# Retention attention and a gated linear unit on one core: stores on ScalarE's queue, a second batch of queries by chunk, output weights in one load, zero products in the waits

## The chip, the core and the metric

The kernel runs on one core of a Trainium2 chip. A core has a matrix engine (TensorE, in the profile PE, with its weight loads as PEld), VectorE (DVE), ScalarE (ACT), GpSimd (POOL) and SyncE (SP), which here only issues transfers. Each engine takes its instructions in the order of the program. Engines wait for each other through semaphores. Sixteen DMA engines move data between HBM and the on-chip memory SBUF. Products of the matrix engine land in PSUM, from where VectorE or ScalarE take them. The metric is the time of one execution in device microseconds; less is better. The time before is 179.71 us, the median of three runs (178.24 to 180.51).

## The reference

Inputs are `q`, `k`, `v` of 8 batches, 8 heads, 576 tokens and 64 values a head, in float32, two 512 x 512 matrices `w_val` and `w_out` and five convolution taps for each of 512 channels.

```python
scores = scale * np.matmul(q, k.transpose(0, 1, 3, 2))
gamma = 1.0 - 2.0 ** (-5.0 - np.arange(H))
Dmat = np.where(rel >= 0, gamma[:, None, None] ** rel[None], 0.0)   # rel = i - j
x = np.matmul(scores * Dmat, v)            # heads side by side: (B, S, 512)
gate_pre = sum(conv_w[k] * xp[:, k:k + S, :] for k in range(5))  # causal, zeros ahead
out = (1 / (1 + np.exp(-gate_pre)) * (x @ w_val)) @ w_out
```

So a linear attention with a decay per head is followed by a gated unit: the gate is a causal convolution over tokens within each channel, the value a full product, and the output again a full product.

## The kernel before, in words

**Chunks.** The tokens of a batch are cut into four chunks of 128 and a tail of 64. Tails of two batches make one chunk. With eight batches there are 36 chunks, in the list `chunks`: batches 0 to 3 by chunk (0 to 15), two tail chunks (16, 17), and the same for batches 4 to 7 (18 to 35).

**Attention of a chunk `t`.** The key tile is cast to bfloat16 (`cast_k`, on GpSimd from chunk 3 on) and turned on the matrix engine with a copy back out of PSUM on VectorE (`turn_k`). Values are cast and weighted with the decay (`cast_v`). Queries are cast (`cast_q`) and turned (`turn_q`, copy on ScalarE unless told otherwise). All turned tiles go through the one PSUM buffer `tps`. `scores` makes the products of keys and queries, `masks` multiplies them with the causal mask on VectorE, `values` adds the products with the values to what `carried` has put there: the products of the queries with the state of the chunks before. `update` adds keys times values to the state in PSUM; `take_state` casts it into SBUF on ScalarE. `take_x` brings the result, with the outgoing decay `gout`, into the tile `xg`.

**Unit `n`.** Two chunks, 2n and 2n + 1, make a unit of the gated part: `conv` (40 small products with diagonal matrices, L379), `gate` (two sigmoids on ScalarE, L387), `value` (two groups of eight products, L394, and the multiplication with the gate on VectorE) and `project` (two groups of four products with `wob`, L405, a copy to SBUF on ScalarE, L408, and a store, L411, or L414 for tails). All these share three PSUM buffers named `g`.

**Loads.** Keys and values come by chunk (`load`, L78 and L81), 256 KB each in pieces of 256 bytes. The queries of batch 0 and of the tails come by chunk as well. The queries of the other batches come as one load of 1 MB (`load_queries`, L94) with pieces of 1 KB: partition p then holds tokens 4p to 4p + 3, so the turned queries have another token order, which `mask_q`, `queries` and `take_x` account for. There are nine buffers for keys and for values (`LA` + 1), two for batch queries.

**Order.** The order is written out by hand (`manual_schedule`): each engine's queue follows the order of the calls. Chunks 0 to 3 with units 0 and 1 stand line by line ahead of a loop (L442 to L531). The loop from L533 runs over `t`: it issues the load of chunk t + 6, casts for later chunks, then `scores` and `masks` of t + 1, `values` of t, in even steps `conv` and `gate` of unit n = t/2 - 1, then `turn_k` of t + 2, half a `value` or `project`, the turned query tiles that `qjobs` lists for this step, the other half, and `carried` and `update` of t + 1. All loads and nearly all stores are issued by SP, so a store that waits for its tile holds up the loads behind it, as does a long issue.

**Zero products.** `keep_warm(n)` issues n products of zeros (L437), 512 columns wide. Before the change they stand only at the very start.

**Output weights.** The convolution leaves half of the channel blocks with their 64-row halves exchanged. `wob` therefore has the rows of `w_out` exchanged in the same way; three loads (L109 to L111) bring the rows to their places, and `prep_wo` (L198) only casts.

Of the kernel before, what the change touches and what calls it, by code (L numbers as in the profile page):

```python
# [21 lines left out]
def kernel(  # L22
# [20 lines left out]
    LA = 8  # L43
    RQ = NCH
    assert D == 64 and DM == H * D and TAIL == 64 and B % GB == 0 and NP == 4
# [24 lines left out]

    with tc.manual_schedule():
# [34 lines left out]

        wof = consts.tile([P, 2, 2, DM], F32, name="wof")
        wo_src = moe_w_out.rearrange("(pr ab hl p) n -> ab hl p pr n", pr=2, ab=2, hl=2)
# [89 lines left out]
        def prep_wo(copy, i):  # L198
            rows, blk, ab = ((slice(0, 64), 0, 0), (slice(64, 128), 0, 1), (slice(0, 64), 2, 1), (slice(64, 128), 2, 0))[i]
            copy(wob[rows, blk:blk + 2], wof[rows, ab])  # L200
# [75 lines left out]
        def masks(t, i):  # L276
            kind, b, c = chunks[t]
            m = mask_t if kind == "tail" else mask if b == 0 else mask_q
# [36 lines left out]
        def take_x(t):  # L315
# [3 lines left out]
            if kind == "full":  # L319
                i0 = c * P  # L320
                if b == 0:
                    nc.vector.tensor_tensor(x[:, bl, :, PAD + i0:PAD + i0 + P], ops[t], gout[:, :, i0:i0 + P], op=ALU.mult)  # L322
                    return
# [76 lines left out]
        def project(n, i):  # L400
            kind, b, c = chunks[2 * n]
            last = n == NT // 2 - 1
            o = ps_g.tile([P, DM], F32, name="g")
            for j in range(NP):
                nc.tensor.matmul(o, lhsT=zsb[n, j // 2][:, j % 2, i * P:(i + 1) * P], rhs=wob[:, j, :],  # L405
                                 start=(j == 0), stop=(j == NP - 1))
            ob = op_sb.tile([P, DM], F32, name="ob")
            nc.scalar.copy(ob, o)  # L408
            if kind == "full":
                c0 = (c + i) * P  # L410
                nc.sync.dma_start(out=out[b, c0:c0 + P, :], in_=ob)  # L411
            else:
                for j in range(2):
                    (nc.scalar if last and j else nc.sync).dma_start(out=out[b + 2 * i + j, NCH * P:S, :], in_=ob[j * TAIL:(j + 1) * TAIL])  # L414
# [8 lines left out]
        for b in range(B - 1, 1, -1):  # L423
            fit = [s for s in range(3, start_of[b] - 1) if s not in qjobs][-RQ:]
            for r, s in enumerate(fit):
                qjobs[s] = [("batch", b, r)]
        qload = {}
# [4 lines left out]
        v_copy, g_copy, s_copy = nc.vector.tensor_copy, nc.gpsimd.tensor_copy, nc.scalar.copy  # L432
        idle = ps_g.tile([P, DM], F32, name="g")

        def keep_warm(n):
            for _ in range(n):
# [87 lines left out]
        cast_k(4)  # L524
        turn_q(("batch", 1, 1), v_copy)
        cast_v(4)
        turn_k(4)
        turn_q(("batch", 1, 2))
        turn_q(("batch", 1, 3), v_copy)
# [3 lines left out]
        for t in range(3, NT + 2):  # L533
            n = t // 2 - 1
            odd = t % 2 == 1
            unit = 2 <= n < NT // 2
# [7 lines left out]
            if t == 3:  # L544
                cast_k(5)
                cast_v(5)
                for job in jobs:
                    cast_q(job)
# [29 lines left out]
            for job in jobs:  # L578
# [37 lines left out]
```

## Time and profile before

| | before |
|---|---|
| median of three runs | 179.71 us (178.24 to 180.51) |
| profiled execution | 179.62 us, span 177.8 us |
| mean granted clock of the matrix engine | 0.936 |
| matrix engine busy | 157.3 us (88%) |
| VectorE, ScalarE, GpSimd busy | 116.2, 89.9, 83.9 us |
| moved by transfers | 40.22 MB, mean 226 GB/s |
| start of unit 1 and of unit 2 (first convolution product in the chain) | 28.11 us, 50.40 us |

The span runs from the first to the last instruction; the time of an execution is a little longer. "Busy" for the matrix engine does not say that it works at its peak. Its granted clock is a share of full speed. The DMA share is the mean share of time in which the sixteen DMA engines have a packet in work, and it can exceed one where packets overlap. In the lists of queues, `SPq` and `ACTq` are the issuing sides of SyncE and ScalarE; the duration is that of the issue, not of the transfer.

### The profile page before, as it was taken

Reading aid. Unit: us, or ns where it says so; the run is one execution under the profiler, and the core shown is the slowest. Engines: PE = TensorE matmul, PEld = TensorE weight load, DVE = VectorE, ACT = ScalarE, POOL = GpSimd, SP = SyncE. Lnnn points to the kernel's source line nnn. Section 1 sums busy time; section 2 is a strip of 40 time slices with the busy share of each in tenths; the row PEclk is TensorE's granted clock in tenths of the full one; section 3 lists DMA queues with packets and bytes.
Section 4 is the critical chain, followed back from the end, with each engine's and each line's share of the span. In section 5 each row is a group of like instructions: output and inputs, shape, how many; then the busy total and the mean of one; then the engine's idle time right before and its main releaser. Section 6 shows DMA issues by size and latency. Waiting matters only on the chain.

```text
span 177.8 us, 5555 instructions
## 1 busy us (share of the span) xinstructions
PE 157.3 (88%) x2267; PEld 115.0 (65%) x2285; DVE 116.2 (65%) x223; ACT 89.9 (51%) x181; POOL 83.9 (47%) x124
## 2 busy tenths in 40 slices
PE   6767759958899999999979989999999999999980
PEld 1445637635586868677666858677777868677640
DVE  5585564337377777876858667776777678876430
ACT  6744226512555565557543645655565654455331
POOL 5349423959153195740547257615765653530000
PEclk9985985885899999999999999999999999999997
DMA  6999997999989899989899999999999988863124
GB/s 134 221 320 220 266 280 154 294 232 270 303 210 297 185 269 226 249 235 205 227 218 273 291 265 250 296 208 223 239 247 246 286 227 188 196 235 119 39 85 118
DMA packets 97063, 40.22 MB, mean 226 GB/s; under 512 B 84218, under 2 KB 91406, under 8 KB 97038
## 3 DMA queue, kind: packets, MB, share of 16 engines
q1 hardware_dynamic: 96848, 39.59, 92.7%
q8 instruction: 18, 0.29, 0.8%
q10 hardware_dynamic: 190, 0.27, 0.6%
q14 instruction: 7, 0.06, 0.1%
HBM read 30.42 MB, written 9.44 MB: 224 GB/s over the span
## 4 chain that ended last, share of the span: by engine, by line
PE 62%; DVE 14%; DMA 12%; ACT 3%; issue 3%; SPq 1%; POOL 1%; ACTq 0%; DVEq 0%; POOLq 0%
PE g L394 15%; PE g L405 14%; DMA fkc<-in_k_dram 12%; PE g L379 12%; PE tps L232 8%; DVE p L280 6%; PE s L270 4%; PE o L312 4%; DVE z L397 4%; PE st L346 2%; PE o L295 1%; DVE kt L240 1%; DVE xg L322 1%; POOL kb L207 1%; ACT qt L254 1%
## 5 line engine op out<-in xcount | busy, mean ns | idle before, releaser
L280 DVE TENSOR_TENSOR p<-s,maskq 128x512 bf16<-128x512 f32 x56 | 38.4, 686 | 16.6 <-PE s L270 16.4
L212 POOL TENSOR_TENSOR vb<-fvc,gin 128x512 bf16<-128x512 f32 x36 | 37.5, 1042 | 10.6 <-DMA fvc<-in_v_dram 6.6
L207 POOL CAST kb<-fkc 128x512 bf16<-128x512 f32 x33 | 20.1, 610 | 45.7 <-DMA fkc<-in_k_dram 41.4
L397 DVE TENSOR_TENSOR z<-gate,g 128x512 bf16<-128x512 f32 x36 | 24.8, 688 | 23.5 <-PE g L394 22.5
L394 PE MATMUL g<-xg,wvb 128*128 128x256 bf16 x288 | 38.2, 280 | 0.0
L408 ACT COPY ob<-g 128x512 f32<-128x512 f32 x36 | 21.1, 585 | 29.4 <-PE g L405 29.1
L405 PE MATMUL g<-wob,z 128*128 128x512 bf16 x126 | 34.1, 388 | 1.5 <-DVE z L397 0.5
L394 PEld LDWEIGHTS <-wvb 128*128 128x128 bf16 x288 | 27.3, 100 | 4.5 <-issue 0.8
L387 ACT ACTIVATE gate<-g 128x512 f32<-128x512 f32 x36 | 19.5, 595 | 19.1 <-PE g L379 19.1
L379 PE MATMUL g<-xg,dg 64*64 64x256 bf16 x720 | 25.4, 287 | 1.5 <-DVE xg L322 1.5
L357 ACT CAST sbd<-st 64x256 bf16<-64x256 f32 x48 | 17.6, 366 | 12.0 <-PE st L346 11.5
L379 PEld LDWEIGHTS <-dg 64*64 64x64 bf16 x720 | 20.4, 112 | 3.5 <-issue 2.2
L225 POOL CAST qb<-fqb 128x512 bf16<-128x512 f32 x28 | 17.0, 613 | 8.1 <-DMA fqb<-in_q_dram 8.1
L254 ACT COPY qtb<-tps 128x512 bf16<-128x512 bf16 x26 | 15.3, 588 | 10.8 <-PE tps L232 10.8
L405 PEld LDWEIGHTS <-z 128*128 128x128 bf16 x144 | 13.0, 100 | 10.8 <-DVE z L397 1.2
L325 DVE TENSOR_TENSOR xg<-o,gout 128x512 bf16<-128x512 f32 x28 | 19.1, 680 | 0.0
L312 PE MATMUL o<-p,vb 128*64 128x128 bf16 x288 | 16.4, 232 | 1.5 <-DVE p L280 1.5
L240 DVE COPY kt<-tps 128x512 bf16<-128x512 bf16 x36 | 15.2, 423 | 3.7 <-PE tps L232 3.5
L232 PE MATMUL tps<-ident,kb 128*128 128x128 bf16 x144 | 14.8, 228 | 2.9 <-POOL kb L207 1.9
L232 PE MATMUL tps<-ident,qb 128*128 128x128 bf16 x144 | 14.4, 224 | 3.0 <-DVE kt L240 1.6
L232 PEld LDWEIGHTS <-qb 128*128 128x128 bf16 x144 | 11.2, 100 | 8.5 <-issue 3.7
L232 PEld LDWEIGHTS <-kb 128*128 128x128 bf16 x144 | 8.6, 100 | 9.2 <-issue 3.2
(60 smaller groups left out, 139.5 us busy)
## 6 DMA issues: line engine op xcount, KB each, us to landing
fkc<-in_k_dram SPq DMA_DIRECT2D x32, 256.0 KB, 5.3
fvc<-in_v_dram SPq DMA_DIRECT2D x32, 256.0 KB, 5.1
out_dram<-ob SPq DMA_DIRECT2D x32, 256.0 KB, 3.9
fqb<-in_q_dram SPq DMA_DIRECT2D x7, 1024.0 KB, 8.4
fqc<-in_q_dram SPq DMA_DIRECT2D x4, 256.0 KB, 5.8
wvf<-in_moe_w_val_dram SPq DMA_DIRECT2D x1, 1024.0 KB, 6.7
fkc<-in_k_dram SPq DMA_DIRECT2D x8, 128.0 KB, 4.0
fqc<-in_q_dram SPq DMA_DIRECT2D x8, 128.0 KB, 4.9
```

Source lines behind the costliest of these rows:

```text
L207: (nc.vector if t < 3 else nc.gpsimd).tensor_copy(kb, loaded["k", *chunks[t]])
L212: nc.gpsimd.tensor_tensor(vb, loaded["v", *chunks[t]], gin[:, chunks[t][2], :].unsqueeze(2).to_broadcast([P, H, D]), op=ALU.mult)
L232: nc.tensor.transpose(ps[:, pr, :], flat[:, pr * P:(pr + 1) * P], ident)
L280: nc.vector.tensor_tensor(p, sps[t][i], m.unsqueeze(1).to_broadcast([P, NP, P]), op=ALU.mult)
L312: nc.tensor.matmul(o[r, pr, :], lhsT=vb[:, 2 * pr + i, :], rhs=pt[t, i][:, pr, :], start=(fresh and pr == 0), stop=(pr == NP - 1), skip_gr ...
L325: nc.vector.tensor_tensor(by_token(x[:, bl, :, PAD + i0:PAD + i0 + P]), ops[t].rearrange("p o (r n) -> p o n r", r=RQ), by_token(gout[:, : ...
L379: nc.tensor.matmul(g[bank][cols, pr, :], lhsT=dg[rows, blk, kk, :], rhs=xs(n, rows, blk, kk), start=(pr == 0 and kk == 0), stop=(pr == 1 a ...
L387: nc.scalar.activation(t, gps[n][i], AF.Sigmoid)
L394: nc.tensor.matmul(vps[:, j, :], lhsT=wvb[:, o, 2 * i + j, :], rhs=xs(n, slice(0, P), o, PAD), start=(j == 0 and o == 0), stop=(j == 1 and ...
L397: nc.vector.tensor_tensor(z, gsb[n][i], vps, op=ALU.mult)
L405: nc.tensor.matmul(o, lhsT=zsb[n, j // 2][:, j % 2, i * P:(i + 1) * P], rhs=wob[:, j, :], start=(j == 0), stop=(j == NP - 1))
L408: nc.scalar.copy(ob, o)
```

## The change

Six things change together.

- Batch 1's queries are loaded by chunk, as batch 0's (`FIRST = 2`). Their turned tiles come two steps ahead of use, one per chunk; the first batch load is that of batch 2.
- The output weights come in one load. `prep_wo` casts one half directly into place (two casts on ScalarE) and the other half into `wsw` on VectorE; four products with a 64 x 64 identity bring that half to the other rows, through the PSUM buffers `g`, and four copies, two on VectorE and two on ScalarE, take it into `wob`.
- Zero products (17 in six calls) stand between the steps of chunks 2 and 3. Each call takes a PSUM buffer `g` in turn. `update` and `take_state` of these chunks move ahead of `values`.
- The first projections move from ahead of the loop into its step 3. In steps with two query jobs the second half of `value` or `project` stands between them.
- Stores are issued by ScalarE, right behind the copy that fills the tile; so are the loads of batch queries from batch 3 on.
- `LA` is 6: seven buffers for keys and values, the loop loads chunk t + 4, and batch loads are issued up to two steps later.

```diff
-    LA = 8
+    LA = 6
+    FIRST = 2
...
-            if kind == "tail" or b == 0:
+            if kind == "tail" or b < FIRST:
                 load_one("q", q, kind, b, c, NCH)
...
-            nc.sync.dma_start(out=t.rearrange("p h r d -> p h (r d)"),
+            (nc.sync if b == FIRST else nc.scalar).dma_start(out=t.rearrange("p h r d -> p h (r d)"),
...
-        nc.sync.dma_start(out=wof[:, 0], in_=moe_w_out.rearrange("(pr ab i) n -> ab i pr n", pr=2, ab=2)[0])
-        nc.sync.dma_start(out=wof[0:64, 1], in_=wo_src[1, 1])
-        nc.sync.dma_start(out=wof[64:128, 1], in_=wo_src[1, 0])
-        load_queries(1)
+        nc.sync.dma_start(out=wof.rearrange("p pr ab n -> p (pr ab) n"), in_=moe_w_out.rearrange("(o i) n -> i o n", i=P))
...
-        def prep_wo(copy, i):
-            rows, blk, ab = ((slice(0, 64), 0, 0), (slice(64, 128), 0, 1), (slice(0, 64), 2, 1), (slice(64, 128), 2, 0))[i]
-            copy(wob[rows, blk:blk + 2], wof[rows, ab])
+        def prep_wo():
+            wsw = consts.tile([P, 2, DM], BF16, name="wsw")
+            v_copy(wsw, wof[:, :, 1, :])
+            s_copy(wob[0:64, 0:2], wof[0:64, :, 0, :])
+            s_copy(wob[64:128, 2:4], wof[64:128, :, 0, :])
+            for pr in range(2):
+                for (r, to, blk, copy) in ((slice(0, 64), slice(64, 128), pr, v_copy),
+                                           (slice(64, 128), slice(0, 64), 2 + pr, s_copy)):
+                    ps = ps_g.tile([P, DM], F32, name="g")
+                    nc.tensor.matmul(ps[to], lhsT=ident[r, r], rhs=wsw[r, pr, :], start=True, stop=True)
+                    copy(wob[to, blk], ps[to])
...
-                nc.sync.dma_start(out=out[b, c0:c0 + P, :], in_=ob)
+                nc.scalar.dma_start(out=out[b, c0:c0 + P, :], in_=ob)
...
-                    (nc.scalar if last and j else nc.sync).dma_start(out=out[b + 2 * i + j, NCH * P:S, :], in_=ob[j * TAIL:(j + 1) * TAIL])
+                    (nc.sync if last and j else nc.scalar).dma_start(out=out[b + 2 * i + j, NCH * P:S, :], in_=ob[j * TAIL:(j + 1) * TAIL])
...
-            if kind == "tail":
+            if kind == "tail" or b < FIRST:
                 qjobs[t - 2] = [("own", t)]
...
+        for r in range(RQ):
+            qjobs.setdefault(start_of[FIRST] - 2 - RQ + 1 + r, []).append(("batch", FIRST, r))
...
         cast_v(2)
+        keep_warm(2)
         scores(2)
         masks(2, 0)
         masks(2, 1)
         carried(2)
+        update(2)
+        take_state(2)
         cast_k(3)
         turn_k(3)
+        keep_warm(2)
         values(2)
         take_x(2)
-        update(2)
-        take_state(2)
         cast_q(("own", 3))
+        keep_warm(4)
         turn_q(("own", 3))
         cast_v(3)
+        keep_warm(2)
         scores(3)
...
         carried(3)
+        update(3)
+        take_state(3)
+        keep_warm(4)
         values(3)
         take_x(3)
-        update(3)
-        take_state(3)
-        for i in range(4):
-            prep_wo(s_copy if i % 2 else v_copy, i)
+        keep_warm(3)
         conv(1)
         gate(1, 0)
         gate(1, 1)
+        prep_wo()
         value(1, 0)
-        for r in range(RQ):
-            cast_q(("batch", 1, r))
+        cast_k(4)
+        cast_q(("own", 4))
+        turn_k(4)
         value(1, 1)
-        project(0, 0)
-        turn_q(("batch", 1, 0))
-        project(0, 1)
...
+        turn_q(("own", 4))
...
-            unit = 2 <= n < NT // 2
+            unit = n != 1 and 0 <= n < NT // 2
...
-            for job in jobs:
+            for i, job in enumerate(jobs):
+                if i == 1 and (unit or t == 4):
+                    project(n, 1) if odd or t == 4 else value(n, 1)
                 turn_q(job)
-            if unit:
-                project(n, 1) if odd else value(n, 1)
-            if t == 4:
-                project(1, 1)
+            if (unit or t == 4) and len(jobs) < 2:
+                project(n, 1) if odd or t == 4 else value(n, 1)
```

More of the change, by code (lines that the diff above doesn't have):

```diff
@@ L69 @@
     NT = len(chunks)
+    v_copy, g_copy, s_copy = nc.vector.tensor_copy, nc.gpsimd.tensor_copy, nc.scalar.copy
     with tc.manual_schedule():
@@ L277, in masks @@
             kind, b, c = chunks[t]
-            m = mask_t if kind == "tail" else mask if b == 0 else mask_q
+            m = mask_t if kind == "tail" else mask if b < FIRST else mask_q
             p = pp.tile([P, NP, P], BF16, name=f"p{i}")
@@ L320, in take_x @@
                 i0 = c * P
-                if b == 0:
+                if b < FIRST:
                     nc.vector.tensor_tensor(x[:, bl, :, PAD + i0:PAD + i0 + P], ops[t], gout[:, :, i0:i0 + P], op=ALU.mult)
@@ L420 @@
         for t, (kind, b, c) in enumerate(chunks):
-            if kind == "tail":
+            if kind == "tail" or b < FIRST:
                 qjobs[t - 2] = [("own", t)]
-        for b in range(B - 1, 1, -1):
-            fit = [s for s in range(3, start_of[b] - 1) if s not in qjobs][-RQ:]
+        for b in range(B - 1, FIRST, -1):
+            fit = [s for s in range(start_of[FIRST] - 1, start_of[b] - 1) if s not in qjobs][-RQ:]
             for r, s in enumerate(fit):
                 qjobs[s] = [("batch", b, r)]
+        for r in range(RQ):
+            qjobs.setdefault(start_of[FIRST] - 2 - RQ + 1 + r, []).append(("batch", FIRST, r))
         qload = {}
@@ L430 @@
             qload.setdefault(max(3, first - LA + 2), []).append(b)
-        v_copy, g_copy, s_copy = nc.vector.tensor_copy, nc.gpsimd.tensor_copy, nc.scalar.copy
-        idle = ps_g.tile([P, DM], F32, name="g")
         def keep_warm(n):
+            idle = ps_g.tile([P, DM], F32, name="g")
             for _ in range(n):
@@ L516 @@
         gate(1, 1)
+        prep_wo()
         value(1, 0)
-        for r in range(RQ):
-            cast_q(("batch", 1, r))
+        cast_k(4)
+        cast_q(("own", 4))
+        turn_k(4)
         value(1, 1)
-        project(0, 0)
-        turn_q(("batch", 1, 0))
-        project(0, 1)
-        cast_k(4)
-        turn_q(("batch", 1, 1), v_copy)
+        turn_q(("own", 4))
         cast_v(4)
-        turn_k(4)
-        turn_q(("batch", 1, 2))
-        turn_q(("batch", 1, 3), v_copy)
+        cast_k(5)
+        for job in qjobs[3]:
+            cast_q(job)
         nc.gpsimd.tensor_copy(mask_t, mask)
@@ L544 @@
             if t == 3:
-                cast_k(5)
                 cast_v(5)
-                for job in jobs:
-                    cast_q(job)
             if ok(t + 3):
@@ L577 @@
                 project(1, 0)
-            for job in jobs:
+            for i, job in enumerate(jobs):
+                if i == 1 and (unit or t == 4):
+                    project(n, 1) if odd or t == 4 else value(n, 1)
                 turn_q(job)
-            if unit:
-                project(n, 1) if odd else value(n, 1)
-            if t == 4:
-                project(1, 1)
+            if (unit or t == 4) and len(jobs) < 2:
+                project(n, 1) if odd or t == 4 else value(n, 1)
             if ok(t + 1):
```

1 line of the change is left out of this document (removed).

## The prediction

> **What bounds the kernel now.** I read the page first, its slices; then the chain of work that ended last.
>
> ```profile
> PEclk9985985885899999999999999999999999999997
> DMA  6999997999989899989899999999999988863124
> ```
>
> Up to slice 11 (about 50 us) the granted clock drops three times; afterwards it is whole. The transfers are nearly full in both stages, until about 155 us. The chain in order of time (start, us, what) gives the stages their lengths:
>
> ```profile
> 7.68 0.76 PE g L437 x3
> ...
> 28.11 2.35 PE g L379 x40
> 30.45 2.66 PE g L394 x16
> ...
> 38.89 0.60 PE s L270 x7
> ...
> 50.40 1.22 PE g L379 x40
> ...
> 82.11 1.22 PE g L379 x40
> ...
> 86.05 5.25 DMA fkc<-in_k_dram
> ...
> 123.55 1.22 PE g L379 x38
> 125.09 0.87 PE g L394 x8
> ...
> 129.60 0.86 PE g L405 x4
> ...
> 162.41 1.22 PE g L379 x40
> ```
>
> L379 is the convolution that opens a unit of two chunks. Unit 1 starts at 28.11 and unit 2 at 50.40, 22.3 us later. Units 11 to 16 (123.55 to 162.41) take 38.86/5 = 7.77 us each: there the matrix engine sets the pace. Units 6 to 11 take 41.44/5 = 8.29 us, and just there the chain runs through key transfers such as the one at 86.05. So 41.44 - 38.86 = 2.6 us of the middle belong to late keys. Why they are late stands in SP's queue (start, us of issuing) and in the windows (last three columns: granted clock, DMA share, GB/s):
>
> ```profile
> 77.90 4.96 SPq L81 DMA_DIRECT2D fqc<-in_q_dram  x2
> 83.29 1.56 SPq L81 DMA_DIRECT2D fvc<-in_v_dram  x2
> 84.96 1.03 SPq L411 DMA_DIRECT2D out_dram<-ob  x2
> 86.05 0.47 SPq L78 DMA_DIRECT2D fkc<-in_k_dram  x1
> ```
> ```profile
> 10.00:12.00 2.00, 1.14 (x20) 0.83 (x20) 1.45 (x3) 0.59 (x1) 1.04 (x1) 0.90 1.06 374
> 24.00:26.00 2.00, 0.94 (x12) 0.69 (x12) 0.60 (x1) 0.91 (x2) 0.00 (x0) 0.81 1.07 333
> 28.00:30.00 2.00, 1.89 (x37) 1.89 (x39) 1.25 (x3) 1.96 (x4) 0.38 (x1) 0.50 0.40 87
> 40.00:42.00 2.00, 1.40 (x17) 1.09 (x15) 1.19 (x3) 0.73 (x2) 1.78 (x4) 0.50 1.35 218
> 84.00:86.00 2.00, 2.00 (x25) 1.76 (x23) 1.07 (x3) 1.04 (x2) 0.49 (x1) 1.00 0.61 135
> ```
>
> The key of 86.05 stands in one queue behind a long issue and two stores, while the transfers run at a share of 0.61. That is what moving the stores can mend. Streams of 256-byte pieces (40 to 42 us: keys and values) move at 218 GB/s, those with the weights' or the batch queries' longer pieces at 333 to 374.
>
> **The first 28 us.** Everything ahead of the second chunk pair is as before. Seventeen zero products are new there: at 0.76/3 = 0.25 us (whole clock) 4.3 us. They stand where the engine waits for copies and masks (24 to 26 us: busy 0.94 of 2.00), so I take 0; without that cover they cost 4.3 us, at half clock twice that. The state update moves ahead of the values; its casts on ScalarE come earlier, nothing later. I leave unit 1's convolution at 28.1.
>
> **Unit 1 and the output weights.** At half clock the convolution takes 2.35 us, at whole clock 1.22; the value products 2.66 against 2 x 0.87. Held warm, both together save 2.35 + 2.66 - 1.22 - 1.74 = 2.05 us. But ScalarE's part changes order:
>
> ```profile
> 28.73 1.99 ACT L200 CAST wob<-wof 64x1024 bf16<-64x1024 f32 x2
> 30.74 1.08 ACT L387 ACTIVATE gate<-g 128x512 f32<-128x512 f32 x2
> 34.02 0.58 ACT L408 COPY ob<-g 128x512 f32<-128x512 f32 x1 [2.20 <-PE g L405]
> ```
>
> Now the gates come first and the two casts (1.99) stand behind them, then a copy out of PSUM (about 0.58, the row of such a copy). The four swap products share three PSUM buffers with the convolution and the value products, so the first value product waits for that copy: convolution done at 29.3, gates to about 30.6, casts to 32.6, copy to 33.2. Two value products (1.74) with the turn of the keys between them end near 35.5; the queries' turn and its copy (another 0.59) give the scores of chunk 4 at about 36.5, against 38.89: -2.4. In exchange the first projections (two of 0.86) and three more turned query tiles (I take 0.40 each, the price of eight small products in the chain at whole clock) come between there and unit 2: +2.9. Over this stretch one window speaks for the clock:
>
> ```profile
> 28.11:50.40 22.29, 18.41 (x194) 12.64 (x199) 10.27 (x19) 10.59 (x21) 12.95 (x20) 0.76 1.05 244
> 123.55:162.41 38.86, 38.60 (x619) 29.27 (x628) 29.90 (x51) 21.47 (x46) 20.40 (x27) 1.00 0.92 224
> ```
>
> The matrix engine is busy 18.41 us at a clock of 0.76. At whole clock that would be 14.0, or 4.4 less; 2.05 of it is counted already. Of the other 2.4 I take 2.0, since the steps are denser now. Unit 2: -2.4 + 2.9 - 2.0 = **-1.5 us**. The ends: -4.4 (all of the clock, the rest hidden) and +2.9 (no clock, no earlier scores).
>
> The clock is where a rule and the rows part. In the rows the clock falls to 0.81 and then 0.50 although the engine is busy about half of the time before; nothing there is idle for long. The Trainium skill's page "TensorE: Matmul & The Clock Gate" ("HAM oscillation") says that only idle gaps of more than about 3.4 us bring the slow clock back. By that rule zero products in short waits would bring nothing; the trace doesn't agree with it.
>
> **Batch 1's queries.** 1.05 MB take 3.1 us at 333 GB/s as one load and 4.8 at 218 by chunk: +1.7 us of transfer time. It costs nothing while the transfers have the idle part of 28 to 30 us (share 0.40, 1.2 us free) and don't wait for 1 MB before chunk 4; if the stream is full throughout, the keys come 1.7 us later. The single load of the output weights moves the same bytes: 0. The lookahead falls from nine buffers to seven, but SP no longer waits for any store, so it can load as soon as a cast frees a buffer: 0. If that cover fails, the 0.52 us per unit of units 6 to 11 would hold in all 16 units, 8.3 us.
>
> **The middle.** With stores out of SP's queue I take the whole **-2.6 us**; ends 0 and -2.6.
>
> **ScalarE's new work.** A store's issue, alone and in pairs with SP's, and the loads' issue (ns, min/median/max):
>
> ```profile
> L411 SPq DMA_DIRECT2D out_dram<-ob x32: 332/395/3783, 40.3 to 168.6; - x32
> ```
> ```profile
> L414 SPq DMA_DIRECT2D out_dram<-ob x6: 513/568/2812, 115.3 to 174.4; - x6
> ...
> L414 ACTq DMA_DIRECT2D out_dram<-ob x2: 483/511/539, 173.1 to 174.4; - x2
> ```
> ```profile
> L78 SPq DMA_DIRECT2D fvc<-in_v_dram x32: 629/1069/5498, 1.9 to 142.4; - x32
> ```
>
> ScalarE is busy 21.47/5 = 4.3 us per unit. Two stores of 0.40 make 5.1 of 7.77, so it doesn't become the bound; but what stands behind a store (a query copy, the gates) comes 0.4 us later. Most of that is hidden in its 3.5 us of idle time per unit. I charge 0.06 us in each of 16 units: **+0.9**; ends 0 (hidden) and 8 (below). A batch load on ScalarE waits for a buffer that was cast two steps before; behind it stand the same copies, and five such issues are few beside 40 stores. At the end the two queues only trade places: 0.
>
> **Sum.** Span 177.8 - 1.5 - 2.6 + 0.9 = 174.6. The profiled run's time is 179.62, 1.8 outside the span, and the median 179.71 is 0.1 above; with 1.9 I forecast **176.5 us**, own range 174.5 to 178.5.
>
> **Rivals.**
> *ScalarE held by its stores (slower).* If an issue on ScalarE must wait for the load that SP is issuing, a store costs 1.07 + 0.40 = 1.47 us, two 2.9 per unit, and the unit's gates stand behind both. ScalarE then needs 7.2 of 7.77 us, the batch loads on top, and any delay shows: at 0.5 us per unit 8 us, so 177.8 - 1.5 + 8 + 1.9 = 186.2. It decides from about 1.1 us per store on. For it: loads that take up to 5.5 us to issue. Against it: the last two pairs, issued at the same moment on both queues, took 483 to 539 ns on ScalarE, no more than SP's own. The Trainium skill's page "Perfetto Trace Analysis" ("DMA Instruction — HWDGE") says that the descriptor generator is locked for exclusive use, which is this rival's mechanism; the paired rows don't show it, and none is in the crowded stage. Chance 0.17.
> *The clock isn't held.* Then 2.05 + 2.0 are lost: 176.5 + 4 = 180.5. For it: the same stretch today has products nearly back to back (1.89 of 2.00) at half clock. Against it: that was already the low state, and the zero products come ahead of it. The clock page's rule gives this case. Chance 0.13.
> *Everything comes.* The whole clock (-4.4), the whole middle (-2.6), no cost on ScalarE: 170.8 + 1.9 = 172.7. For it: the transfers have idle stretches to fill. Against it: the shared PSUM buffers in unit 1 and the 2.9 us of work moved behind the scores. Chance 0.18.
> The forecast has 0.52.
>
> **From these the numbers.** About 2% is what a measurement of this kernel tells from no change: 176.1 and 183.3 us. The forecast's range lies across the first bound: 0.24 faster, 0.28 same. With the rivals: faster 0.24 + 0.18 = 0.42, same 0.28 + 0.13 = 0.41, slower 0.17. The range reaches down to the fast rival with some room, 171.5, and up past the cold clock to 183; most of the slow rival stays outside.
>
> **What would show it.** Unit 1's convolution at 1.2 us for a held clock; unit 2's start near 49; the spacing of units 6 to 11 at 7.8; no SP wait on ScalarE; store issues on ScalarE around 0.4 us; PE idle per unit unchanged. It is wrong if ScalarE's issues last over 1 us in the middle, if keys are still on the chain there, or if unit 2 starts later than 50.4.

## The result, and the profile after

The changed kernel takes 192.59 us (median of four runs, 191.95 to 194.22) against 180.11 us of the kernel before beside it (178.24 to 182.46): a ratio of 1.074, 95% interval 1.062 to 1.086. The forecast was 176.5 us. The profiled execution has a span of 190.2 us, 12.4 more than before.

First the slices of the page of the changed kernel, clock and transfers as before:

```profile
PEclk9995899999999889999999969999999999999997
DMA  6999989899999969999999998999879403113023
```

The clock is held through the first 50 us but for slices 4 and 5. It falls again at slices 14, 15 and 24 (62 to 71 and 109 to 114 us), where the matrix engine now stands still for microseconds. So the zero products and the denser start did what they should, and the loss lies elsewhere. The chain of waits, in order of time (start, us, what), shows where:

```profile
30.18 1.34 PE g L386 x40
31.52 1.07 ACT gate L394 x2
32.59 0.92 ACT wob L200
33.53 1.04 ACT wob L201
34.59 0.59 ACT wob L207
35.22 1.03 PE g L401 x8
...
52.84 9.10 DMA fvc<-in_v_dram
62.77 0.37 ACT sbd L364
63.17 0.61 ACT gate L394
...
70.88 1.22 PE g L386 x40
...
99.77 8.28 DMA fkc<-in_k_dram
108.88 0.37 ACT sbd L364
109.28 0.61 ACT gate L394
...
120.71 6.90 DMA fvc<-in_v_dram
128.44 0.37 ACT sbd L364
128.83 0.61 ACT gate L394
...
135.04 1.22 PE g L386 x40
...
179.81 1.24 PE g L386 x40
```

L386 opens a unit (L379 before). Unit 2 begins at 50.05 us in the timeline (50.33 before), unit 11 at 134.97 (123.47), unit 17 at 179.74 (167.83). So 11.8 of the 12.4 us are lost between units 2 and 11; from unit 11 to 16 it takes 39.29 against 38.87. Three times a transfer of keys or values of 7 to 9 us is followed by state casts (`sbd`) and a gate on ScalarE. But these casts read PSUM and need neither that key nor that value tile. ScalarE's timeline of the changed kernel shows what stands between (start, us, line; in brackets the idle time ahead and what ended it):

```profile
57.49 0.59 ACT L415 COPY ob<-g 128x512 f32<-128x512 f32 x1
62.02 0.34 ACTq L418 DMA_DIRECT2D out_dram<-ob  x1
62.40 0.74 ACT L364 CAST sbd<-st 64x256 bf16<-64x256 f32 x2 [4.32 <-DMA fvc<-in_v_dram]
63.17 1.08 ACT L394 ACTIVATE gate<-g 128x512 f32<-128x512 f32 x2
```

The copy that fills the tile is done at 58.08. Its store is issued at 62.02 only, and everything behind it on ScalarE waits with it. The load that ends this wait is in SP's timeline:

```profile
52.84 1.10 SPq L81 DMA_DIRECT2D fvc<-in_v_dram  x1
54.03 1.33 SPq L81 DMA_DIRECT2D fkc<-in_k_dram  x1
```

52.84 + 9.10 = 61.94: the store starts 0.08 us after the values of chunk 11 have landed, with which it has nothing to do. The other holds look the same: at 108.13 a store was ready for 4.07 us and starts 0.08 us after the key of 99.77 has landed (99.77 + 8.28 = 108.05). The row of these issues shows that the issue itself is cheap (min/median/max ns, first and last start):

```profile
L418 ACTq DMA_DIRECT2D out_dram<-ob x32: 338/339/1016, 39.5 to 180.7; - x32
```

What the store waits for is in the built program. There SP and ScalarE together have eight semaphores on which their transfers report that they have landed, DMAHW0 to 7, given out in turn in one order for both engines, which is fixed before the run. A transfer may start only when the one eight places before it, which uses the same semaphore, has landed. The places around the held store:

```
place  engine   transfer               semaphore
40     SP       values of chunk 11     DMAHW0
41     SP       keys of chunk 12       DMAHW1
42     SP       values of chunk 12     DMAHW2
43     ScalarE  queries of batch 4     DMAHW3
44     SP       keys of chunk 13       DMAHW4
45     SP       values of chunk 13     DMAHW5
46     ScalarE  store of unit 2, 1st   DMAHW6
47     SP       keys of chunk 14       DMAHW7
48     ScalarE  store of unit 2, 2nd   DMAHW0
```

Place 48 waits for its tile and for DMAHW0, that is for the values of chunk 11. On SP such a wait holds only loads. On ScalarE it holds state casts, gates and query copies. Summed over the 38 stores on ScalarE, the time from the end of the instruction ahead to the issue is 13.2 us, about the span lost. Six holds of 0.46 to 4.07 us make 12.0 of it, and each ends within 0.08 us of a landing; one batch load on ScalarE is held by 1.8 us more. The list of waits of the changed kernel (us in total, times, longest) names the loads in which this wait ends, and who waits behind:

```profile
ACT sbd L364 <- DMA fvc<-in_v_dram: 5.2, 2, 4.3
ACT sbd L364 <- DMA fkc<-in_k_dram: 4.4, 1, 4.4
...
PE g L401 <- ACT gate L394: 9.9, 4, 4.5
...
DVE z L404 <- ACT gate L394: 12.5, 4, 5.3
```

A reader who goes by the releaser alone would look for a state cast that needs a key. The Trainium skill's page "Perfetto Trace Analysis" ("DMA Instruction — HWDGE") says that the reported start of a transfer's issue is when all its semaphores are satisfied; the rows agree, since the hold of 3.9 us is no part of the 0.34 us.

### The profile page after: what moved, and what is told of

It reads as the page before. It is cut to its first block, busy times and chain, and to the rows that moved or that the text cites. A ratio compares the mean times of both kernels' runs of the same rounds, so it can differ in the third digit from the quotient of the medians.

```text
span 190.2 us, 5636 instructions
## 1 busy us (share of the span) xinstructions
PE 163.1 (86%) x2306; PEld 116.0 (61%) x2306; DVE 116.3 (61%) x222; ACT 92.9 (49%) x185; POOL 83.5 (44%) x124
## 4 chain that ended last, share of the span: by engine, by line
PE 60%; DMA 21%; ACT 7%; DVE 4%; issue 2%; ACTq 1%; SPq 1%; POOL 0%; POOLq 0%; DVEq 0%
PE g L401 14%; DMA fvc<-in_v_dram 11%; PE g L412 11%; DMA fkc<-in_k_dram 10%; PE g L386 9%; PE tps L239 7%; PE s L277 5%; PE o L319 5%; PE g L445 3%; PE st L353 3%; PE o L302 2%; ACT qt L261 2%; DVE p L287 2%; ACT ob L415 2%; ACT gate L394 2%
## 5 line engine op out<-in xcount | busy, mean ns | idle before, releaser
L219 POOL TENSOR_TENSOR vb<-fvc,gin 128x512 bf16<-128x512 f32 x36 | 37.7, 1048 | 13.2 <-DMA fvc<-in_v_dram 9.8
L287 DVE TENSOR_TENSOR p<-s,maskq 128x512 bf16<-128x512 f32 x48 | 32.9, 686 | 13.1 <-PE s L277 12.9
L412 PE MATMUL g<-wob,z 128*128 128x512 bf16 x144 | 37.1, 384 | 0.3 <-DVE z L404 0.3
L386 PE MATMUL g<-xg,dg 64*64 64x256 bf16 x720 | 24.3, 279 | 0.8 <-DVE xg L329 0.8
L386 PEld LDWEIGHTS <-dg 64*64 64x64 bf16 x720 | 19.5, 109 | 3.2 <-issue 1.8
L261 ACT COPY qtb<-tps 128x512 bf16<-128x512 bf16 x24 | 14.1, 587 | 9.7 <-ACT ob L415 3.3
L232 POOL CAST qb<-fqb 128x512 bf16<-128x512 f32 x24 | 14.8, 616 | 5.1 <-DMA fqb<-in_q_dram 5.1
L332 DVE TENSOR_TENSOR xg<-o,gout 128x512 bf16<-128x512 f32 x24 | 16.3, 681 | 0.0
L319 PE MATMUL o<-p,vb 128*64 128x128 bf16 x288 | 15.8, 230 | 0.6 <-DVE p L287 0.6
L287 DVE TENSOR_TENSOR p<-s,mask 128x512 bf16<-128x512 f32 x16 | 10.6, 685 | 8.5 <-PE s L277 8.5
```

The lines of the kernel that those rows point to most:

```text
L219: nc.gpsimd.tensor_tensor(vb, loaded["v", *chunks[t]], gin[:, chunks[t][2], :].unsqueeze(2).to_broadcast([P, H, D]), op=ALU.mult)
L261: copy(dst, ps)
L319: nc.tensor.matmul(o[r, pr, :], lhsT=vb[:, 2 * pr + i, :], rhs=pt[t, i][:, pr, :], start=(fresh and pr == 0), stop=(pr == NP - 1), skip_gr ...
L386: nc.tensor.matmul(g[bank][cols, pr, :], lhsT=dg[rows, blk, kk, :], rhs=xs(n, rows, blk, kk), start=(pr == 0 and kk == 0), stop=(pr == 1 a ...
```

## The experiments

Theory A: stores on ScalarE wait for loads through the shared semaphores, and the gates wait with them. Rivals: the issue itself is dear on ScalarE; stores and batch loads on one ring hold each other; some other part of the change is slow. "Waits" in the tables is the sum just described over the stores on ScalarE (a store that isn't held counts 0.03).

### One part back, and one part alone

Stores back on SP in the changed kernel:

```diff
-                nc.scalar.dma_start(out=out[b, c0:c0 + P, :], in_=ob)
+                nc.sync.dma_start(out=out[b, c0:c0 + P, :], in_=ob)
```

(and the same for tails.)

> The changed kernel with only the stores given back to SyncE's queue; batch queries stay on ScalarE. Theory A (ScalarE is held: a store waits on a completion semaphore that it shares with a key or value load still on its way, and the state casts and gates stand behind it; in the changed kernel's trace the held stretches before stores add up to about 12 us): the holds vanish, about 179 us, ratio to before 0.98 to 1.01. Theory B (seven buffers instead of nine and the second batch by chunk starve the casts): stays at 188 to 193.

181.49 us, ratio 1.009 (1.004 to 1.013). Without stores on ScalarE 11 us are back.

The kernel before with that one edit the other way round, `nc.scalar` for its stores:

> The kernel before with only its stores moved to ScalarE. In this program most stores share their completion semaphore with an older store, not with a load. Theory A: few holds, so 177 to 183 us, ratio 0.98 to 1.02. Rival (each issue on ScalarE costs by itself, as the prediction's slow rival has it): 184 to 192.

183.85 us, ratio 1.019 (1.010 to 1.028), waits 3.5 us. ScalarE's timeline of this run at the store that is held in the changed kernel:

```profile
59.35 0.59 ACT L408 COPY ob<-g 128x512 f32<-128x512 f32 x1
59.97 0.34 ACTq L411 DMA_DIRECT2D out_dram<-ob  x1
60.35 0.75 ACT L357 CAST sbd<-st 64x256 bf16<-64x256 f32 x2 [0.41 <-ACT ob L408]
```

The store follows its copy at once. Stores on ScalarE alone don't explain 12 us.

Batch loads back on SP in the changed kernel, the stores staying on ScalarE:

```diff
-            (nc.sync if b == FIRST else nc.scalar).dma_start(out=t.rearrange("p h r d -> p h (r d)"),
+            nc.sync.dma_start(out=t.rearrange("p h r d -> p h (r d)"),
```

> The changed kernel with the batch query loads given back to SyncE; stores stay on ScalarE. Theory A: stores still share semaphores with loads, 185 to 193 us. Theory C (the batch loads on ScalarE, waiting for their buffer, hold it): 178 to 182.

181.53 us, ratio 1.012 (1.003 to 1.020), waits 2.9 us. Theory A, as it then stood, was missed: the stores are on ScalarE and hardly wait. The time is what theory C expected, that batch loads waiting for a buffer hold ScalarE. But the first run has them on ScalarE as well and takes 1.009, so they don't do it alone.

Both back on SP:

> The changed kernel with stores and batch loads both on SyncE: what is left is the by-chunk second batch, one weight load, zero products, seven buffers. Theory A: 177 to 181 us; unit 1's convolution still near 1.3 us and unit 2's start near 50. Theory B: 186 or more.

181.81 us, ratio 1.014 (1.010 to 1.018). So neither costs 1.4%, either one about 1%, both 7.4%. The two act together. What is left beside them, 1.4%, is a loss too.

### What makes a store's load young

Two runs were to move a store's place against the loads. The first adds a load of 16 bytes per loop step on SP to the kernel with the batch loads on SP; the second is its control with the stores on SP:

```diff
+            for _ in range(PADS.get(t, 0)):
+                i = 4 * len(padded)
+                padded.append(t)
+                nc.sync.dma_start(out=spare[:, i:i + 4], in_=moe_conv_w[0:1, i:i + 4])
```

> The kernel with only the batch loads back on SP's queue and the stores on ScalarE's took 181.5 us, with 2.9 us of waiting ahead of its stores. Here it gets one more load of 16 bytes per loop step on SP (30 in all), into a tile that nobody reads. Theory A (a store on ScalarE waits until the transfer eight places before it in the common order of SP's and ScalarE's transfers has landed): the small loads move each store's place, so that younger key and value loads stand eight places before them; from the landing times of the 181.5 us run I work out about 14 to 19 us of waiting ahead of stores, so about 190 (186 to 197) us. Rival 1 (only the batch loads on ScalarE's ring slow things, or the issue itself does): 181 to 183.5 us, waits ahead of stores about 3 us. Rival 2 (late keys by the small loads themselves): the control with the stores on SP rises as much.

183.79 us, ratio 1.012 (0.999 to 1.026), waits 1.2 us.

> The same 30 small loads on SP, with the stores on SP too and the batch loads on ScalarE (that kernel took 181.5 us without them). They prices the small loads alone: each is an issue of some 0.4 us on SP, 12 us of issuing over 130 us. Theory A and rival 1: 181 to 184 us. Rival 2: as much more as in the run with the stores on ScalarE.

184.74 us, ratio 1.025 (1.015 to 1.035). With the stores on SP the small loads cost 1.6% (1.009 without them), with the stores on ScalarE nothing (1.012), and the stores don't wait.

One store per unit, so that fewer transfers lie between:

```diff
-                nc.scalar.dma_start(out=out[b, c0:c0 + P, :], in_=ob)
+                if i == 1:
+                    nc.scalar.dma_start(out=out[b, c * P:(c + 2) * P, :].rearrange("(i p) n -> p i n", p=P), in_=obs[n])
```

> The changed kernel, with stores and batch loads still on ScalarE's queue, but one store of 256 rows (512 KB) per unit in place of two of 128 rows. The bytes are the same. Theory A: one transfer fewer per unit puts older transfers eight places before a store; by the landing times of the changed kernel the waits ahead of stores fall from about 11 to about 1 us, so 180 to 184 us. Rival (a batch load and stores on one ring compete, or a store's issue is held by SP's issue): half as many issues but the same bytes, 187 to 193 us.

190.85 us, ratio 1.060 (1.052 to 1.069), waits 14.9 us. Both expectations of theory A missed, in opposite directions, and 190.85 us lies in the range of this run's rival, by which a batch load and stores on one queue compete. I had shifted places and kept the landing times. But the order itself changes with what stands in SP's queue: read from the built programs, the youngest load that stands eight places before a store of unit n (units 2 to 11) is of chunk 2n + 12 in the changed kernel, 2n + 12 with one store per unit, but 2n + 7 with the batch loads on SP and 2n + 6 with the small loads. In the program a store of unit n is called in step 2n + 3, where chunk 2n + 7 is loaded. So with stores and batch loads both gone from its queue, nothing holds SP but free buffers, its loads stand up to five chunks further ahead in the common order, and a store waits for a load that was issued a few microseconds before. This is theory A as mended. The next four runs test it.

One row of each unit's second store on SP, so that SP waits for that tile again:

```diff
-                nc.scalar.dma_start(out=out[b, c0:c0 + P, :], in_=ob)
+                r0 = 1 if i == 1 else 0
+                nc.scalar.dma_start(out=out[b, c0 + r0:c0 + P, :], in_=ob[r0:P])
+                if r0:
+                    nc.sync.dma_start(out=out[b, c0:c0 + 1, :], in_=ob[0:1])
```

> The changed kernel, with stores and batch loads still on ScalarE's queue, but one row of 128 (2 KB of 256 KB) of each unit's second store is issued by SP. So SP waits once per unit for the filled tile, as it did before, and moves almost nothing more. Theory A, mended after the runs with the small loads and with one store per unit (SP, with neither stores nor batch loads in its queue, is placed several chunks further ahead in the common order of SP's and ScalarE's transfers, so that eight places before a store on ScalarE stands a young load, which has not landed): with the row on SP's queue no store has a load younger than chunk 2n + 7 eight places before it (in the changed kernel up to 2n + 12), the waits ahead of stores fall from 13 to under 3 us, and the time to 181.5 to 183.5 us. Rival (a batch load and stores that share ScalarE's ring hold each other, or a batch load on a second ring slows SP's loads): nothing of it changes, 188 to 194 us.

300.08 us, ratio 1.661 (1.648 to 1.673), which neither theory expects. Its stores wait 18.7 us, but transfers are slow throughout, so this decides nothing between the two; the reason, stores of 127 rows, stands in the last section.

Batch loads on GpSimd:

```diff
-            (nc.sync if b == FIRST else nc.scalar).dma_start(out=t.rearrange("p h r d -> p h (r d)"),
+            (nc.sync if b == FIRST else nc.gpsimd).dma_start(out=t.rearrange("p h r d -> p h (r d)"),
```

> The changed kernel with the batch loads (of batches 3 to 7) issued by GpSimd in place of ScalarE; the stores stay on ScalarE. SP is still alone with the key and value loads. Theory A: SP still runs ahead, eight places before the stores of units 8 and 9 stand loads of chunks 2n + 10 to 2n + 12, so waits ahead of stores of 5 us or more in all and 185 to 192 us. Rival (it needs the batch loads on ScalarE's own ring beside the stores): 181 to 183 us, waits under 3 us.

195.30 us, ratio 1.080 (1.072 to 1.088), waits 15.6 us, a little more than expected. The batch loads needn't be on ScalarE's ring; it is enough that they aren't in SP's queue. Not all of this is young loads: two holds, 3.6 us together, wait for older stores that took 8.4 and 9.0 us to land.

Three buffers for keys and values in place of seven:

```diff
-            load_one("k", k, kind, b, c, LA + 1)
+            load_one("k", k, kind, b, c, 3)
```

(and the same for `v`.)

> The changed kernel with three buffers for keys and for values in place of seven; the calls stay where they are. Theory A: with three buffers SP can't run as far ahead (eight places before a store stand loads of chunk 2n + 9 at most, in place of 2n + 12), so the waits ahead of stores shrink, and the time falls although there is less room for loads: 184 to 189 us. Rival (fewer buffers only take lookahead away): later keys, 193 us or more.

183.51 us, ratio 1.019 (1.007 to 1.030), waits 5.1 us. Taking away four of seven buffers makes the changed kernel 9 us faster, since SP can't run as far ahead. The hold at unit 2 is still there, behind the values of chunk 11 as in the changed kernel; the later ones are nearly gone:

```profile
57.35 0.59 ACT L415 COPY ob<-g 128x512 f32<-128x512 f32 x1
61.34 0.34 ACTq L418 DMA_DIRECT2D out_dram<-ob  x1
```

Everything on SP with nine buffers and `LA = 8` as before the change:

> The changed kernel with stores and batch loads both on SP (that took 181.8 us against 179.4 of the kernel before) and with nine buffers and loads six slots ahead, as before the change. The forecast took the smaller lookahead as free, at a price of 8.3 us without its cover. If the 2.4 us that this kernel stays above the one before come from the lookahead: 179 to 180 us. If they come from the transfers (batch 1's queries in short pieces, 1.7 us more of transfer time): 181 to 183 us.

180.57 us, ratio 1.001 (0.995 to 1.007), against 1.014 with seven. The smaller lookahead is the 1.4%.

### The decisive pair

Sixteen rows of each unit's second store on SP, 112 on ScalarE (`r0 = 16` above); batch loads stay on ScalarE:

> The run with one row of a store on SP's queue (300 us) told nothing of the waits: its stores of 127 rows moved 10 to 11 packets of 2 KB per microsecond, where a store of 128 rows moves up to 95, so one DMA engine carried them. Here SP issues 16 rows (32 KB) of each unit's second store and ScalarE the other 112; stores of one row and of the first half stay whole otherwise, and batch loads stay on ScalarE's queue. Theory A (SP with neither stores nor batch loads runs ahead, and a store on ScalarE then waits for a load that was issued shortly before): SP waits once per unit for the filled tile, no store has a load younger than chunk 2n + 7 eight places before it, waits ahead of stores under 4 us in all, 181 to 184 us. Rival (stores and batch loads on ScalarE's queue hold each other whatever SP does): 188 to 194 us.

185.09 us, ratio 1.030 (1.019 to 1.041); the profiled execution took 498 us and the other three 184.9 to 185.1, so its profile isn't used. The same kernel again:

> The run with 16 rows of each unit's second store on SP took 185 us, but its profile was a disturbed execution of 498 us. This is the same kernel again, for its profile. Theory A: waits ahead of stores under 4 us in all, and the time 184 to 186 us.

184.97 us, ratio 1.033 (1.022 to 1.044), waits 3.0 us. ScalarE's timeline of this run at the second store of unit 2:

```profile
59.01 0.59 ACT L415 COPY ob<-g 128x512 f32<-128x512 f32 x1
59.63 0.38 ACTq L419 DMA_DIRECT2D out_dram<-ob  x1
60.05 0.74 ACT L364 CAST sbd<-st 64x256 bf16<-64x256 f32 x2 [0.45 <-ACT ob L415]
```

Stores and batch loads are on ScalarE as in the changed kernel, 1/16 of the stores' bytes has moved, and ten of the 13 us of waiting and 7.6 us of the time are gone (192.59 to 184.97; the ratio falls from 1.074 to 1.033). The time is 1 us above the first expectation, and 1.9% above the kernel with everything on SP; where that goes wasn't looked into.

The kernel before with stores and batch loads (from batch 3 on) on ScalarE, nothing else changed; ahead of it the batch loads alone:

```diff
-            nc.sync.dma_start(out=t.rearrange("p h r d -> p h (r d)"),
+            (nc.sync if b <= 2 else nc.scalar).dma_start(out=t.rearrange("p h r d -> p h (r d)"),
```

> The kernel before with only the batch loads of batches 3 to 7 issued by ScalarE; stores stay on SP. Theory A: SP still waits for the stores' tiles and doesn't run ahead, and the batch loads on ScalarE cost what their issue costs (0.4 us each, five of them): ratio 0.995 to 1.01. Rival (a batch load on a second ring slows SP's loads by itself): late keys, 1.02 or more.

182.48 us, ratio 1.019 (1.005 to 1.033). Between the two expectations; SP doesn't run ahead here, as its stores hold it. A part of the 1.9% can be read in ScalarE's timeline, a wait that the batch load took along:

```profile
85.51 0.59 ACT L254 COPY qt<-tps 128x512 bf16<-128x512 bf16 x1 [0.34 <-PE tps L232]
90.01 0.37 ACTq L94 DMA_DIRECT2D fqb<-in_q_dram  x1
90.43 0.74 ACT L357 CAST sbl<-st 64x256 bf16<-64x256 f32 x2 [4.33 <-POOL qb L225]
```

The batch load waits 3.9 us for GpSimd's cast that frees its buffer, and another one at 106.82 waits 1.3 us. How much of this reaches the end of the span wasn't tried.

> The kernel before with stores and batch loads (of batches 3 to 7) both issued by ScalarE and nothing else of the change. Each alone made it 1.9% slower. Theory A (with neither in its queue SP runs ahead, and stores wait for young loads): eight places before the stores of units 6 to 10 stand loads of chunks 2n + 9 to 2n + 13, so waits ahead of stores of 8 us or more in all, and a ratio of 1.05 to 1.10, more than the sum of the two parts (1.038). Rival (the two parts simply add): 1.03 to 1.045.

200.01 us, ratio 1.119 (1.109 to 1.129), more than expected. Stores wait 13.3 us, and batch loads are held as well (three of them by 2.5 to 3.4 us). ScalarE's timeline of this run shows its longest hold:

```profile
93.26 0.59 ACT L408 COPY ob<-g 128x512 f32<-128x512 f32 x1
98.98 0.34 ACTq L411 DMA_DIRECT2D out_dram<-ob  x1
99.42 1.08 ACT L387 ACTIVATE gate<-g 128x512 f32<-128x512 f32 x2 [5.57 <-DMA fkc<-in_k_dram]
```

The tile is ready at 93.85, the store leaves at 98.98, 0.07 us after the key issued at 90.36 has landed. So the two moves alone, without the other four parts of the change, cost 11.9%, where their single costs add to 3.8%.

The runs side by side, by how far SP is ahead:

| kernel | youngest load eight places before a store, units 2 to 11 | waits, us | ratio |
|---|---|---|---|
| before, both on ScalarE | 2n + 13 | 13.3 | 1.119 |
| changed | 2n + 12 | 13.2 | 1.074 |
| changed, one store per unit | 2n + 12 | 14.9 | 1.060 |
| changed, batch loads on GpSimd | 2n + 11 | 15.6 | 1.080 |
| changed, three buffers | 2n + 9 | 5.1 | 1.019 |
| before, stores on ScalarE | 2n + 9 | 3.5 | 1.019 |
| changed, batch loads on SP | 2n + 7 | 2.9 | 1.012 |
| changed, 16 rows on SP | 2n + 6 | 3.0 | 1.033 |
| changed, batch loads and small loads on SP | 2n + 6 | 1.2 | 1.012 |

The first column is a coarse measure. The hold of 3.9 us at unit 2 of the changed kernel waits for a load of chunk 2n + 7, no younger by this count than the youngest in the run with 2.9 us of waits; what counts in the end is when that load was issued and how long it took.

### The clock and a better version

The zero products alone in the kernel before, at the same places:

> The kernel before with the 17 zero products alone, at the places where the change has them; update and take_state stay where they were. By the forecast's step: unit 1's convolution at about 1.3 us in place of 2.35 us and a start of unit 2 about 4 us earlier (2.05 + 2.0). If the middle keeps its pace, 175.7 us against 179.4; if the transfers set the pace behind it, as the run with stores and batch loads both on SP suggests (start of unit 2 2.3 us earlier, time 1.4% longer), then 179 to 180 and units 5 to 11 slower than 8.25 us. I take 178.5 (175.5 to 181). Rival (the rule that only an idle gap of microseconds lowers the clock): 2.35 us stays and the time rises by up to 4 us.

180.04 us, ratio 0.998 (0.993 to 1.003). The windows of the kernel before and of this one (after the span: busy us and number of PE, PEld, DVE, ACT, POOL; then clock, DMA share, GB/s):

```profile
28.00:34.00 6.00, 5.84 (x63) 4.45 (x64) 2.62 (x5) 3.76 (x6) 4.32 (x9) 0.66 0.76 191
34.00:42.00 8.00, 5.11 (x52) 3.39 (x49) 2.89 (x6) 2.98 (x6) 5.61 (x9) 0.81 1.28 255
```
```profile
28.00:34.00 6.00, 4.68 (x72) 3.44 (x72) 3.06 (x5) 3.80 (x6) 4.57 (x7) 1.00 0.79 195
34.00:42.00 8.00, 5.10 (x45) 3.25 (x43) 3.41 (x7) 2.25 (x4) 4.99 (x10) 0.79 0.92 228
```

The clock is held where they stand (0.66 to 1.00) and falls behind them (0.79). What unit 1's products gain, ScalarE's casts take back (the two casts of the output weights, 1.99 us, stand on the chain from 30.13): unit 2 starts at 50.66. The clock alone is worth nothing here.

The changed kernel with stores on SP, batch loads on ScalarE and nine buffers was to beat both:

> The changed kernel with its stores back on SP (181.5 us) and with nine buffers and loads six slots ahead, as before the change. Batch loads stay on ScalarE's queue. The nine buffers brought the kernel with everything on SP from 1.4% above the kernel before to 0.1%. If the same holds here: ratio 0.99 to 1.00, 178.5 to 180 us, and the start of unit 2 that came 1.6 us earlier is then what remains. If the transfers set the pace of the middle: 1.00 to 1.01.

182.53 us, ratio 1.015 (1.004 to 1.026). Missed: nine buffers help with everything on SP and not here. No run was faster than the kernel before.

## Why the prediction was wrong, by its steps

**ScalarE's new work, the step that failed.** I took a store on ScalarE as its issue, 0.40 us, 0.06 us of it on the path of each unit. The issue's price held: from unit 11 to 16, where hardly a store waits, the changed kernel takes 39.29 against 38.87 us, 0.08 us a unit. What I left out is that a moved store takes its waits along: not only that for its tile, which ScalarE has just filled, but that for the transfer eight places before. On SP that wait was there as well, in front of loads. I named what is queued behind a store on ScalarE (query copies, gates) and asked only how long the store's issue would take. The span is 15.6 us over the forecast's 174.6: 1.2 us of it by unit 2, 13.8 between units 2 and 11, 0.6 behind. The 13.2 us of waits, where I had charged 0.9, are the largest part, and give the miss its sign.

**The slow rival** (186.2 us, chance 0.17) had the engine and the waiting gates right and the mechanism wrong: an issue on ScalarE doesn't wait for SP's issue. Row L418 gives 339 ns as the median and 338 as the least, in the crowded stage as at the end. The Trainium skill's "Perfetto Trace Analysis" has the lock of the descriptor generator inside the reported time; in this trace such a wait is at most 1016 - 339 = 0.7 us, for the slowest of 32. My argument against the rival, the last two pairs of stores, looked at the issue time too, so it refuted the price and couldn't see the hold. The 1.1 us a store from which the rival was to decide don't follow from its rows: ScalarE's 3.5 us of idle time a unit leave 1.7 for each of two stores.

**SP "can load as soon as a cast frees a buffer: 0".** This was the step that made the damage possible. I took SP's freedom as harmless; it is what puts young loads eight places before the stores. The price of a lookahead too small that I named was the smaller thing: with all on SP, seven buffers cost 1.4% against 0.1% with nine, about 2.3 us of the 8.3 I had given as the bound. That batch 1's queries by chunk cost nothing beside it fits the run with nine buffers.

**The middle, -2.6.** With stores out of SP's queue and batch loads in it (the two runs with waits of 2.9 and 3.5 us) units 6 to 11 take 40.66 us in place of 41.43: 0.8 of the 2.6 came. The rest didn't come with the stores out of the queue, and what else makes keys late stays open: in the kernel before, GpSimd's key casts wait 41.4 us for keys, and in the changed kernel with the batch loads on SP still 25.7 (from the two lists of waits):

```profile
POOL kb L207 <- DMA fkc<-in_k_dram: 41.4, 18, 6.3
```
```profile
POOL kb L214 <- DMA fkc<-in_k_dram: 25.7, 9, 5.7
```

**The first 28 us and unit 1** went as forecast. Unit 1's convolution took 1.34 us in place of 2.35, and the order on ScalarE was as worked out: 5.0 us from the convolution's start to the end of the copy that the first value product waits for (30.18 to 35.18; forecast 28.1 to 33.2). The zero products cost nothing that can be told: unit 1 starts between 28.2 and 30.4 us in the profiles that have them (but for that of 498 us), and between 27.8 and 30.5 in four kernels whose code up to there is that of before. From unit 1 to unit 2 it takes 19.9 us in the changed kernel, where 20.8 was forecast. In seven profiles of kernels with the changed start this stretch takes 19.0 to 19.9 us and in the others 22.3 to 24.7; what decides that wasn't tried.

**The clock's rule.** In the kernel before, the matrix engine has no idle stretch of over 1.3 us in the first 50 us, and the granted clock falls three times there. The rule in the Trainium skill's "TensorE: Matmul & The Clock Gate" ("HAM oscillation") is to have no idle gaps of more than about 3.4 us. The trace doesn't agree that this is enough, and neither does the run with the zero products alone: short waits were filled there, and the clock of 28 to 34 us went from 0.66 to 1.00. No time was gained, as that rule would have it, but for another reason, ScalarE's casts. What decides the clock stays open.

**Why the two moves need each other** is shown by the counts and by the runs with three buffers and with 16 rows. Not shown is how much of each hold is the load's age and how much its length: the two longest in the changed kernel (3.9 and 4.1 us) wait for loads of 9.1 and 8.3 us, issued within 0.3 us of a batch load of 1 MB, where keys and values issued away from batch loads (60 to 80, 106 to 120 and 128 to 145 us) land in 3.7 to 7.2 us. The run with the batch loads on GpSimd keeps both; its longest hold, 8.4 us, is again for a load issued within 0.3 us of a batch load. The run with three buffers changes the age and leaves the batch loads where they were.

## What to carry to other kernels

A transfer moved to another engine takes all its waits along, also the one for the semaphore that it shares with transfers of other engines; look in the built program for what it will wait for, and put what is behind it on that engine into the price. Before freeing a load queue of its last wait, ask what that wait held back: an engine that runs ahead fills the shared places that others then stand in line for. And when a wait in the profile names a transfer that the instruction doesn't read, look for a transfer's issue between the two.

## What the runs showed of the hardware

A store of 127 rows runs on one DMA engine. In the run with one row of a store on SP, ScalarE's other 127 rows move in packets of 2 KB at 10 to 11 per microsecond, one after the other (0.085 us each), where a store of 128 rows reaches over 100 in a microsecond. Loads that land beside it wait for that one engine, as the windows of this run and of the changed kernel show (columns as above):

```profile
115.00:119.00 4.00, 2.12 (x12) 1.27 (x10) 1.11 (x2) 1.84 (x5) 0.00 (x0) 0.50 0.15 46
```
```profile
115.00:119.00 4.00, 4.00 (x80) 3.17 (x79) 2.62 (x5) 1.21 (x3) 2.17 (x3) 1.00 0.82 204
```

A DMA share of 0.15 of sixteen engines at 46 GB/s, with the matrix engine waiting: 300 us. The Trainium skill's "DMA: Bandwidth & Descriptors" ("Why a DMA increments its semaphore by 16 and not by 1") states it: a transfer uses the largest number of engines, up to 16, that divides its rows, and 127 rows leave one. The trace agrees. With 112 and 16 rows, both multiples of 16, it is gone.

And fewer buffers can be faster: three in place of seven took 9 us off the changed kernel.
